# A timetable for the K stage, row tiles for half of Q, and the first denominators moved into gate/up

## The chip, the cores and the metric

The kernel runs on one core of a Trainium2 chip. The metric is the device time of one execution in microseconds; lower is better. A profile is one execution, of which the span (first to last instruction) is 1.7 to 1.8 us shorter than the device time. PE is TensorE, ACT is ScalarE, DVE is VectorE, POOL is GpSimd, SP is SyncE.

## The reference

```python
x  = A_x                                   # 1 x 2048 x 576, bf16
xn = layernorm(x)
# linear attention: 32 heads of 18
q, k, v = split_heads(xn @ wqkv)
phi = lambda t: where(t > 0, t + 1, exp(t)) + 1e-6
num = phi(q) @ (phi(k)^T v);  den = phi(q) . sum(phi(k)) + 1e-6
attention = (num / den) @ wo
# feed-forward with a gate
ffn = (gelu(x @ w_gate) * (x @ w_up)) @ w_down     # of xn
out = x + attention + ffn
```

## The kernel before

PE goes through these stages in order: K (layer norm, transposes, the K projection and G = xn^T phi(k), tile by tile), Q, then for each quarter of the rows gate/up and down. The first down stage begins with M, ten small matmuls that multiply the attention's kv by wo. PE writes into PSUM, which the kernel holds as one tile of 8 banks of 512 columns; a bank can be written again when ACT and DVE have read it. The change touches K, Q and the first gate/up stage.

In the K loop each tile n does the following; steps of tiles ahead are mixed in, and two tiles share one rstd from tile 7 on:

```python
for n in range(1, NS):
    if n > 1:
        k_half(n, 0); k_half(n, 1)               # PE: 10 matmuls of 288 columns
    if n + 1 < NS: tp_all(n + 1)                 # ACT: copy the transposes
    if n + 2 < NS and (n + 2 < PAIRED or n % 2 == 1):
        ln_rstd(n + 2, min(1 if n + 2 < PAIRED else 2, NS - n - 2))
    if n + 2 < NS: ln_norm(n + 2)                # DVE
    k_read(n, 0); k_read(n, 1)                   # ACT relu, DVE max, out of PSUM
    k_finish(n)                                  # ACT exp, POOL add -> pk
    ln_stats(...)                                # DVE
    if n >= GLAG: g_accumulate(n - GLAG, G_A)    # PE
    if n + 2 < NS: transposes(n + 2)             # PE
    if n in (NS - 2, NS - 1): q_unit(...)        # the first two units of Q
    # ... loads ...
```

phi is computed in two pieces that POOL adds. Both K and Q take the pieces from one small set of buffers, and Q has 20 units (4 row blocks x 5 groups of heads):

```python
def phi_tiles():
    e = awork.tile([P, D], F32, name="phi_e", tag="phi_e", bufs=3)
    a = awork.tile([P, D], F32, name="phi_a", tag="phi_a", bufs=2)
    return e, a

def q_unit(i):
    # ... 5 matmuls of 512 columns into one PSUM bank ...
    if i % 3 != 2:
        # ACT relu of the bank; DVE max of the bank into a; ACT exp; POOL add -> pqT
    else:
        # ACT exp of the bank; DVE max of the bank into a; DVE joins them -> pqT
```

The contraction is 576 rows, 4.5 times the array. Gate/up already uses row tiles so that the half block costs half a slot: two outputs are worked on at once, one in rows 0 to 63 of the array and one in 64 to 127, and they change places between `p1` and `p2`. A do-nothing instruction on another engine, the relay, passes on that the other row tile has written:

```python
def p1(self):
    for kt in (4, 0, 1, 2, 3):
        self.mm(0, LO, kt, kt == 4, False)
        last = self.mm(1, HI, kt, kt == 4, False)
    self.turn = self.relay.nop()      # waits for `last`
def p2(self):                         # first matmul waits for self.turn
    for kt in range(4): ...
```

The relay runs on GpSimd for all blocks of gate/up but the first two. That was so before the change already.

Of the kernel before, what the change touches and what calls it, by code (L numbers as in the profile page):

```python
# [40 lines left out]
PAIRED = 7  # L41
# [15 lines left out]
def kernel(  # L57
# [45 lines left out]

    def load_w(which):
        c = slice(which * D, (which + 1) * D)
        nc.sync.dma_start(wqkv_sb[:, 0:4, c], A_wqkv[0:512, c].rearrange("(kt p) c -> p kt c", p=P))
        nc.sync.dma_start(wqkv_sb[0:HP, 4, c], A_wqkv[512:576, c])

# [89 lines left out]
    ln_done = [0]  # L198

    def ln_stats(halves):  # L200

        while ln_done[0] < min(halves, 2 * NS):
            n, a_ = divmod(ln_done[0], 2)
            if a_ == 0:
                stats_t[n] = asmall.tile([P, 2, nc.vector.BN_STATS_DIM], F32, name="stats")
            nc.vector.bn_stats(out=stats_t[n][:, a_, :], in_=x_sb[:, n, a_ * HALF:(a_ + 1) * HALF])  # L206
            if a_ == 1:
                nc.vector.bn_aggr(out=mv[:, n, :], in_=stats_t.pop(n)[:])
            ln_done[0] += 1

    def ln_rstd(n, cnt=1):
        r = rstd[:, n:n + cnt]
        nc.scalar.activation(out=r, in_=mv[:, n:n + cnt, 1], func=ACT.Ln, bias=eps_ln[:], scale=1.0)  # L213
        nc.scalar.activation(out=r, in_=r, func=ACT.Exp, scale=-0.5)  # L214

    def ln_norm(n, dup=None):
        nc.vector.tensor_scalar(  # L217
            out=xn[:, n, 0:D], in0=x_sb[:, n, :], scalar1=mv[:, n, 0:1], scalar2=rstd[:, n:n + 1],
            op0=ALU.subtract, op1=ALU.mult,
        )  # L220
        (dup or nc.gpsimd).tensor_copy(out=xn[:, n, D:640], in_=xn[:, n, 512:D])
# [7 lines left out]
    def tp_copy(n, k0, k1, copy):  # L229
        copy(out=xnT[:, k0:k1, n * P:(n + 1) * P], in_=tp_bank[:, k0:k1, :])  # L230
# [20 lines left out]
    def k_read(n, hf):  # L251
        if hf == 0:
            k_ea[n] = phi_tiles()
        e, a = k_ea[n]
        hs = slice(hf * HALF, (hf + 1) * HALF)
        src = ps_all[:, k_bank(n, hf), :HALF]
        nc.scalar.activation(out=e[:, hs], in_=src, func=ACT.Relu, scale=-1.0)
        nc.vector.tensor_scalar(
            out=a[:, hs], in0=src, scalar1=0.0, scalar2=EPS_ATT, op0=ALU.max, op1=ALU.add,
        )  # L260

    def k_finish(n):
        e, a = k_ea.pop(n)
        nc.scalar.activation(out=e[:], in_=e[:], func=ACT.Exp, scale=-1.0)  # L264
        nc.gpsimd.tensor_tensor(out=pk[:, n, :], in0=e[:], in1=a[:], op=ALU.add)  # L265
# [10 lines left out]
    def g_accumulate(n, pieces):  # L276
# [7 lines left out]

    vcopy, acopy = nc.vector.tensor_copy, nc.scalar.copy

    G_COPIES = {
        3: [(0, G_A, 0, acopy), (0, G_A, 1, vcopy), (2, G_A, 0, acopy), (2, G_A, 1, vcopy)],
        5: [(1, G_A, 0, acopy), (2, G_A, 2, vcopy)],
        6: [(4, G_A, 2, acopy), (1, G_A, 1, vcopy)],  # L290
        7: [(4, G_A, 0, acopy), (4, G_A, 1, vcopy)],
        14: [(3, G_B, 0, acopy), (3, G_B, 1, vcopy)],
    }

    def tp_all(n):
        tp_copy(n, 0, KT, acopy)

    q_next = [0]
# [4 lines left out]
    def q_unit(i):  # L303
# [3 lines left out]
        cs = slice(sc * SC, (sc + 1) * SC)  # L307
        ps = ps_all[:rows, q_banks.next(), :]
        for kt in range(KT):
            nc.tensor.matmul(  # L310
                ps, lhsT=wqkv_sb[:, kt, q0:q0 + rows], rhs=xnT[:, kt, cs],
                start=(kt == 0), stop=(kt == KT - 1),
            )
        e, a = phi_tiles()
# [51 lines left out]

    def den_mm(sc, c, bank):
# [3 lines left out]
        d = dwork.tile([P, SC], F32, name="den_sb", tag="den_sb", bufs=5)  # L371
        if sc == 0:
            nc.scalar.activation(out=d[:rows, :], in_=ps, func=ACT.Identity, bias=eps_att[:rows, :], scale=1.0)
        else:
            nc.vector.tensor_scalar_add(out=d[:rows, :], in0=ps, scalar1=EPS_ATT)
        den_sb[c] = d

    def den_norm(sc, c, q, pieces):
        w = SC // pieces
        rows = DH * HCH[c]  # L380
        d = den_sb[c][:rows, q * w:(q + 1) * w]
# [8 lines left out]

    ln_stats(2)
    ln_rstd(0)
    ln_stats(3)
    ln_norm(0, nc.vector)
    transposes(0)
    ln_stats(4)
    tp_copy(0, 0, KT, vcopy)
    ln_rstd(1)
    k_half(0, 0)
    ln_norm(1)  # L400
    transposes(1)
    ln_stats(6)
    k_half(0, 1)
    k_read(0, 0)
    tp_all(1)
    ln_rstd(2)
    ln_stats(7)
    k_half(1, 0)
    ln_norm(2)
    k_read(0, 1)  # L410
    k_finish(0)
    transposes(2)
    k_half(1, 1)
    ln_stats(9)


    for n in range(1, NS):

        if n > 1:
            k_half(n, 0)  # L420
            k_half(n, 1)
        if n + 1 < NS:
            tp_all(n + 1)
        if n + 2 < NS and (n + 2 < PAIRED or n % 2 == 1):
            ln_rstd(n + 2, min(1 if n + 2 < PAIRED else 2, NS - n - 2))
        if n + 2 < NS:
            ln_norm(n + 2)
        k_read(n, 0)
        k_read(n, 1)
        k_finish(n)  # L430
        ln_stats(2 * (n + 4) + (1 if n < PAIRED - 4 else 2))
        if n >= GLAG:
            g_accumulate(n - GLAG, G_A)
        if n + 2 < NS:
            transposes(n + 2)
        if n in (NS - 2, NS - 1):
            q_unit(q_next[0])
            q_next[0] += 1
        if n == 2:
            load_x(8, 4)  # L440
        elif n == 3:
            load_x(12, 4)
        elif n == 5:
            load_w(0)
        elif n == 6:
            load_w(2)
        elif n == 7:
            load_wo()
        elif 8 <= n < 8 + NWBUF:
            load_gu(n - 8, 0)  # L450
            load_gu(n - 8, 1)
# [8 lines left out]
    for i in range(2, NSC * NCH):  # L460
        if i == 8:
            q_banks = _Ring([2, 3, 4, 5, 6, 7])
        q_unit(i)
        if i < 2 + GLAG:
            g_accumulate(NS - GLAG + i - 2, G_A)
        for kt, pieces, part, copy in G_COPIES.get(i, ()):
            g_copy(kt, pieces, part, copy)
        if i == 10:
            z_stage()
        if 5 <= i < 13:  # L470
            for n in (2 * (i - 5), 2 * (i - 5) + 1):
                g_accumulate(n, G_B)
        if 13 <= i < 13 + NCH:
            den_mm(0, i - 13, q_banks.next())
        if i == 17:
            kv_stage()
    scales = []
# [17 lines left out]



    LO, HI = slice(0, HP), slice(HP, P)
    SYNC = mybir.DependencyInfo(mybir.DependencyClass.Sync, mybir.DependencyReason.DATA)
    banks = _Ring(list(range(8)))  # L500

    class _Unit:


        def __init__(self, outs, lhs, rhs, relay=nc.gpsimd):
            self.outs, self.lhs, self.rhs, self.relay = outs, lhs, rhs, relay

        def mm(self, i, rows, kt, start, stop):
            return nc.tensor.matmul(  # L509
                self.outs[i], lhsT=self.lhs(i, rows, kt), rhs=self.rhs(i, rows, kt),  # L510
                start=start, stop=stop, skip_group_check=True,
            )

        def p1(self):
            for kt in (4, 0, 1, 2, 3):
                self.mm(0, LO, kt, kt == 4, False)
                last = self.mm(1, HI, kt, kt == 4, False)
            self.turn = self.relay.nop()
            tc.add_manual_dep(self.turn.ins, last.ins.name, SYNC, reason="the row tiles take turns on a bank")

        def p2(self):
            for kt in range(4):
                m = self.mm(1, LO, kt, False, kt == 3)
                if kt == 0:
                    tc.add_manual_dep(m.ins, self.turn.ins.name, SYNC, reason="the bank's other row tile has written")
                self.mm(0, HI, kt, False, kt == 3)

    def gu_pair(sc, k):
# [19 lines left out]
        if sc == 0 and k >= 1:  # L548
            load_wd_slice()
        for i, (b, u) in enumerate(units):  # L550
# [3 lines left out]
            nc.vector.tensor_tensor(out=hT[:, GUB * k + i, :], in0=ps_all[:, b[1], :], in1=gl[:], op=ALU.mult)  # L554

    m_banks = _Ring(list(range(2, 8)))

    def m_stage(chunks):
        for c in chunks:
            rows = DH * HCH[c]  # L560
            for hf in range(2):
                b = m_banks.next()
                hs = slice(hf * HALF, (hf + 1) * HALF)
                nc.tensor.matmul(  # L564
                    ps_all[:rows, b, :HALF], lhsT=kvT[:rows, c, :rows], rhs=wo2[:rows, c, hs], start=True, stop=True,
                )
                nc.scalar.copy(out=m_sb[:rows, c, hs], in_=ps_all[:rows, b, :HALF])

    def down_tile(sc, j, hooks):
# [4 lines left out]
        for hf in range(2):  # L574
            hs = slice(hf * HALF, (hf + 1) * HALF)
            todo = hooks.pop(0) if hooks else {}
            acc = ps_all[:, banks.next(), :HALF]
            for f in range(NF):
                if f in todo:
                    todo[f]()  # L580
# [14 lines left out]
    for sc in range(NSC):  # L595
        for k in range(NF // GUB):
# [3 lines left out]
            if den_jobs:  # L600
# [4 lines left out]
        hooks = [{6 * c_: (lambda c_=c_: m_stage((c_,))) for c_ in range(NCH)} if sc == 0 else {}]  # L605
        if sc + 1 < NSC:
            for c_ in range(NCH):
                def dn(c=c_, nsc=sc + 1):
                    den_mm(nsc, c, banks.next())
# [34 lines left out]
```

## Time and profile before

| | before |
|---|---|
| device time, median of the first 3 runs | 528.93 us (528.82 to 529.08) |
| PE busy | 520.7 us, 99% of the span |
| PE work after 12 us without a listed wait | all of it |
| Q unit 0 starts | 45.22 us |
| gate/up starts (first row-tiled matmul) | 77.75 us |
| first matmul of the M stage, at the start of down | 147.95 us |
| last matmul ends | 524.01 us |

The four times at the bottom are positions of PE in the trace. Here is the stretch at the end of K and the start of Q, from the chain in order of time of the kernel before (start, length, what):

```profile
45.38 1.09 PE ps_all L310 x5
46.47 1.23 PE ps_all L238 x10
47.70 0.98 PE ps_all L280 x10
48.68 2.17 PE ps_all L310 x10
50.86 0.99 PE ps_all L280 x10
51.84 1.09 PE ps_all L310 x5
52.94 0.99 PE ps_all L280 x10
```

Every piece starts where the one above ends, and each is a PE piece: Q unit 0 (L310), K of tile 15 (L238), G of tile 13, units 1 and 2, G of tile 14, unit 3, G of tile 15. No other engine holds PE up.

### The profile page before, as it was taken

To read this page: it belongs to the slowest core of one execution; us is meant where nothing else is said; L and a number is where in the kernel's file an instruction comes from. 1 tells how busy PE (TensorE), PEld (TensorE's weight loads), DVE (VectorE), ACT (ScalarE), POOL (GpSimd) and SP (SyncE) were. 2 spreads that over 40 slices of the span, in tenths; PEclk is the share of its full clock that TensorE was granted. 3 is DMA by queue.
4 is the path that set the end of the run, shared out by engine and by line. 5 is a ranking of instruction groups with operands and counts; after the bars stand their busy time and mean duration, and the time that the engine had idled before them with its cause. 6 is when DMAs were issued, how large, how long until landed. Compare 5 with 4: busy or idle time off the path is not lost.

```text
span 527.1 us, 10752 instructions
## 1 busy us (share of the span) xinstructions
PE 520.7 (99%) x4532; PEld 326.2 (62%) x4532; DVE 248.7 (47%) x408; ACT 152.8 (29%) x288; POOL 70.3 (13%) x83
## 2 busy tenths in 40 slices
PE   7999999999999999999999999999999999999997
PEld 5887666666677764444577744444777544445775
DVE  7885766774348613334368233433485233333101
ACT  5887783332330003233200023323000132322000
POOL 4666542210002100000011000000021000000000
PEclk9999999999999999999999999999999999999999
DMA  8900006999510025555400055455100345540000
GB/s 277 278 10 1 1 1 173 265 269 265 154 46 12 24 79 154 158 145 156 135 12 13 12 168 158 141 158 154 46 24 12 102 143 159 149 136 1 12 12 22
DMA packets 98810, 55.85 MB, mean 106 GB/s; under 512 B 5322, under 2 KB 98378, under 8 KB 98762
## 3 DMA queue, kind: packets, MB, share of 16 engines
q1 hardware_dynamic: 98762, 55.17, 36.2%
q8 instruction: 35, 0.57, 0.5%
q14 instruction: 13, 0.11, 0.1%
HBM read 52.79 MB, written 2.36 MB: 105 GB/s over the span
## 4 chain that ended last, share of the span: by engine, by line
PE 98%; DVE 1%; ACT 1%; DMA 0%; issue 0%
PE ps_all L509 53%; PE ps_all L581 27%; PE ps_all L310 4%; PE ps_all L586 4%; PE ps_all L280 4%; PE ps_all L238 3%; PE ps_all L227 1%; PE ps_all L370 1%; DMA x_sb<-in_A_x_dram 0%; ACT xnT L230 0%; PE ps_all L564 0%; PE ps_all L358 0%; DVE xn L217 0%; DVE stats L206 0%; ACT rstd L213 0%; ACT rstd L214 0%
## 5 line engine op out<-in xcount | busy, mean ns | idle before, releaser
L509 PE MATMUL ps_all<-xnT,wg 64*128 64x512 bf16 x1152 | 272.8, 376 | 0.0
L509 PE MATMUL ps_all<-xnT,wu 64*128 64x512 bf16 x1152 | 268.4, 376 | 0.0
L554 DVE TENSOR_TENSOR hT<-ps_all,gl 128x512 bf16<-128x512 f32 x144 | 99.5, 691 | 166.3 <-ACT gl L553 165.9
L553 ACT ACTIVATE gl<-ps_all 128x512 f32<-128x512 f32 x144 | 86.0, 597 | 313.5 <-PE ps_all L509 289.2
L581 PE MATMUL ps_all<-wd_sb,hT 128*128 128x288 bf16 x1152 | 147.0, 286 | 0.0
L509 PEld LDWEIGHTS <-wg 64*128 64x128 bf16 x1152 | 108.2, 94 | 62.6 <-issue 0.3
L509 PEld LDWEIGHTS <-wu 64*128 64x128 bf16 x1152 | 107.4, 94 | 61.8
L581 PEld LDWEIGHTS <-hT 128*128 128x128 bf16 x1152 | 112.3, 98 | 30.7 <-issue 1.3
L384 DVE RECIPROCAL den_sb<-den_sb 126x128 f32<-126x128 f32 (+1 forms) x80 | 68.3, 911 | 0.5
L387 POOL TENSOR_TENSOR pqT<-pqT,den_sb 126x512 bf16<-126x512 bf16 (+3 forms) x25 | 24.1, 964 | 298.5 <-DVE den_sb L384 295.2
L509 PE MATMUL ps_all<-xnT,wr 64*128 64x512 bf16 x288 | 60.6, 376 | 0.0
L589 DVE TENSOR_TENSOR res<-ps_all,x_sb 128x288 bf16<-128x288 f32 x32 | 14.6, 457 | 87.5 <-PE ps_all L586 87.5
L509 PEld LDWEIGHTS <-wr 64*128 64x128 bf16 x288 | 17.1, 94 | 16.3 <-issue 1.1
L586 PE MATMUL ps_all<-m_sb,pqT 126*128 126x288 bf16 (+1 forms) x160 | 24.9, 286 | 0.0
L310 PE MATMUL ps_all<-xnT,wqkv_sb 128*126 128x512 bf16 (+1 forms) x100 | 24.4, 380 | 0.0
L265 POOL TENSOR_TENSOR hT<-phi_e,phi_a 128x576 bf16<-128x576 f32 x16 | 22.4, 1402 | 8.9 <-ACT phi_e L264 4.9
L280 PE MATMUL ps_all<-hT,xn 128*128 128x288 bf16 (+3 forms) x192 | 23.6, 266 | 0.0
L238 PE MATMUL ps_all<-wqkv_sb,xnT 128*128 128x288 bf16 x160 | 22.5, 286 | 0.7 <-DVE xnT L230 0.6
L280 PEld LDWEIGHTS <-xn 128*128 128x128 bf16 (+1 forms) x192 | 18.2, 101 | 4.5
L320 POOL TENSOR_TENSOR pqT<-phi_e,phi_a 126x512 bf16<-126x512 f32 (+1 forms) x14 | 17.7, 1267 | 15.5 <-DVE phi_a L318 11.8
L586 PEld LDWEIGHTS <-pqT 126*128 126x128 bf16 (+1 forms) x160 | 15.5, 97 | 4.1
L238 PEld LDWEIGHTS <-xnT 128*128 128x128 bf16 x160 | 15.0, 98 | 4.6 <-DVE xnT L230 0.8
(58 smaller groups left out, 201.3 us busy)
## 6 DMA issues: line engine op xcount, KB each, us to landing
wg<-in_B_w_gate_dram SPq DMA_DIRECT2D x72, 256.0 KB, 2.9
wu<-in_B_w_up_dram SPq DMA_DIRECT2D x72, 256.0 KB, 3.4
wd_sb<-in_B_w_down_dram SPq DMA_DIRECT2D x12, 432.0 KB, 4.4
wr<-in_B_w_gate_dram SPq DMA_DIRECT2D x72, 32.0 KB, 2.7
wr<-in_B_w_up_dram SPq DMA_DIRECT2D x72, 32.0 KB, 3.0
out_dram<-res SPq DMA_DIRECT2D x15, 144.0 KB, 1.8
x_sb<-in_A_x_dram SPq DMA_DIRECT2D x3, 576.0 KB, 6.6
wqkv_sb<-in_A_wqkv_dram SPq DMA_DIRECT2D x2, 576.0 KB, 8.9
```

Of the source, the lines that this page charges most:

```text
L238: nc.tensor.matmul(ps_all[:, k_bank(n, hf), :HALF], lhsT=xnT[:, kt, n * P:(n + 1) * P], rhs=wqkv_sb[:, kt, D + hf * HALF:D + (hf + 1) * HALF],
L265: nc.gpsimd.tensor_tensor(out=pk[:, n, :], in0=e[:], in1=a[:], op=ALU.add)
L280: nc.tensor.matmul(ps_all[:m, b, col:col + w], lhsT=xn[:, n, j0:j0 + m], rhs=pk[:, n, d0:d0 + w], start=(n == 0 and col == 0), stop=(n == ...
L310: nc.tensor.matmul(ps, lhsT=wqkv_sb[:, kt, q0:q0 + rows], rhs=xnT[:, kt, cs], start=(kt == 0), stop=(kt == KT - 1),)
L320: nc.gpsimd.tensor_tensor(out=pqT[:rows, c, cs], in0=e, in1=a, op=ALU.add)
L384: nc.vector.reciprocal(out=d[:, h:h + P], in_=d[:, h:h + P])
L387: nc.gpsimd.tensor_tensor(out=pqT[:rows, c, cols], in0=pqT[:rows, c, cols], in1=d, op=ALU.mult)
L509: return nc.tensor.matmul(self.outs[i], lhsT=self.lhs(i, rows, kt), rhs=self.rhs(i, rows, kt), start=start, stop=stop, skip_group_check=True,)
L553: nc.scalar.activation(out=gl[:], in_=ps_all[:, b[0], :], func=ACT.Gelu_apprx_tanh)
L554: nc.vector.tensor_tensor(out=hT[:, GUB * k + i, :], in0=ps_all[:, b[1], :], in1=gl[:], op=ALU.mult)
L581: nc.tensor.matmul(acc, lhsT=hT[:, f, j * P:(j + 1) * P], rhs=wd_sb[:, f, hs], start=(f == 0), stop=False,)
L586: nc.tensor.matmul(acc, lhsT=pqT[:rows, c, ts_], rhs=m_sb[:rows, c, hs], start=False, stop=(c == NCH - 1),)
```

## The change

The intent is to make PE's work shorter in Q and its start denser:

- K gets a timetable. Each step has a time for each tile, and all steps are issued in the order of these times. rstd is no longer paired.
- The second half of Q is done in five pairs of units with the row tiles of gate/up, with relays on SP.
- The first six denominators leave Q (and one the first down stage) and are done in three row-tiled pairs inside gate/up.
- To make room, the second part of G and the z and kv stages (which make the denominators' and M's weights) move forward to units 5 to 8 of Q, and G of tiles 14 and 15 comes one unit later.
- The relays on GpSimd stay as they are.

The diff, cut to its core:

```diff
+    TILE = 2.5
+    STEPS = [
+        (lambda n: ln_half(n, 0), [3.02, 3.99, 6.44, 7.41, 9.44]),
+        ...
+        (lambda n: k_half(n, 0), [6.86, 8.09, 10.30, 13.01, 15.56]),
+        ...
+        (k_exp, [8.73, 11.12, 13.29, 15.61, 18.10]),
+        (k_add, [9.59, 11.73, 14.01, 16.29, 19.88]),
+    ]
+    todo = [(at(times, n), step, n) for n in range(NS) for step, times in STEPS]
+    todo += [(at(STEPS[7][1], NS - 1) - 0.01, q_unit, 0), (at(G_AT, NS - GLAG) - 0.01, q_unit, 1)]
+    todo += [(at(STEPS[-1][1], 4 + n) + 0.01, lambda n: nc.gpsimd.memset(pqT[HP:P, NCH - 1, ...], 0.0), n)
+             for n in range(2)]
+    ...
+    for _, step, n in sorted(todo, key=lambda x: x[0]):
+        step(n)
...
-    for i in range(2, NSC * NCH):
+    for i in range(2, 2 * NCH):
...
+    q_banks = _Ring(list(range(8)))
+    for k, items in enumerate([[(2, 0), (2, 1)], [(2, 2), (2, 3)], [(2, 4), (3, 4)], [(3, 0), (3, 1)], [(3, 2), (3, 3)], None]):
+        if items:
+            u = q_pair(items)
+            u.p1()
+        if prev:
+            prev[1].p2()
+            ...  # q_phi of the two units
...
+    DEN_FROM = 2
+    DEN_PAIRS = [[(0, 0), (0, 1)], [(0, 2), (0, 3)], [(0, 4), (1, 4)]]
...
-        if sc == 0:
-            nc.scalar.activation(out=d[:rows, :], in_=ps, func=ACT.Identity, bias=eps_att[:rows, :], scale=1.0)
-        else:
-            nc.vector.tensor_scalar_add(out=d[:rows, :], in0=ps, scalar1=EPS_ATT)
+        nc.vector.tensor_scalar_add(out=d[:rows, :], in0=ps, scalar1=EPS_ATT)
```

## The prediction

> **What bounds the kernel now.** I read the page's busy shares and chain first, then the waits of PE, the chain in order of time, and the timeline of three stretches. The first lines are the page's first part and the chain that ended last.
>
> ```profile
> PE 520.7 (99%) x4532; PEld 326.2 (62%) x4532; DVE 248.7 (47%) x408; ACT 152.8 (29%) x288; POOL 70.3 (13%) x83
> PE 98%; DVE 1%; ACT 1%; DMA 0%; issue 0%
> ```
>
> PE is busy 99% of the span, and the chain that sets the end runs on it for 98%. All the waits of PE that the trace lists come to 3.1 us:
>
> ```profile
> PE ps_all L132 <- POOL ident masks.py:199: 1.4, 1, 1.4
> PE ps_all L227 <- DVE xn L217: 1.1, 1, 1.1
> PE ps_all L238 <- DVE xnT L230: 0.6, 1, 0.6
> ```
>
> So almost nothing is to be had by removing listed waits. What can shorten the time is less PE work, or a denser start, where PE also has dead time that is put down to pipelining. The chain in order of time shows the K stage (columns: start, length, what):
>
> ```profile
> 12.19 1.23 PE ps_all L238 x10
> 13.42 0.98 PE ps_all L280 x10
> ...
> 21.91 0.52 PE ps_all L227 x5
> 22.43 1.25 PE ps_all L238 x10
> 23.68 0.98 PE ps_all L280 x10
> 24.66 0.33 PE ps_all L227 x5
> ```
>
> A tile of K is transposes (L227), ten K matmuls (L238) and ten accumulations of G (L280): at best 0.28 + 1.23 + 0.98 = 2.49 us. In every second tile the transposes take 0.52 instead of 0.28, because they wait for a norm that waits for the paired rstd. G of tile 0 starts at 13.4, of tile 12 at 44.4: 12 tiles in 31.0 us, 2.58 each, so 1.1 us above the best in steady state. Before 12 us PE is mostly idle: from its first transpose at 5.31 to 12.03 it does four groups of transposes and four K halves, 4 x 0.28 + 4 x 0.61 = 3.6 us of work in 6.7 us. So a perfect start could give some 3.1 us, a perfect steady state 1.1.
>
> **What the Trainium skill says.** (1) "TensorE: Matmul & The Clock Gate", Back-to-back issue gap: an isolated 512-column matmul takes about N / 2.4 + 2.5, some 216 ns, and a stream about 131. Here the starts of plain 512-column matmuls (L310) and those of pairs of row tiles (L509) stand 216 to 217 ns apart (648 matmuls of L509 in 70.2 us is 216.7 ns a pair). The trace agrees with the first figure, not with the second. (2) The same page, Weight-path perf modes: fast weight load needs 128 columns. The trace agrees: 98 ns for 128 columns (L581), 132 ns for 126 (L310). (3) "TensorEngine Tiling (Array Packing)", Gotcha 1: PSUM Pressure: row tiles may not use one PSUM bank at once and software must order them. That is what the relay between the two halves of a unit is for. (4) "PSUM — Partial Sum Buffer", PSUM bank collisions: no two engines may be in one bank (and quadrant) together. The trace agrees in effect: in Q, DVE's read of a bank starts only after ACT's (relu 46.57 to 47.17, maximum from 47.27), so a bank of Q comes free some 1.7 us after its last matmul was issued: 0.25 + 0.6 + 0.1 + 0.7.
>
> **The change part by part.**
>
> Row-tiled second half of Q. Now 10 units of 5 matmuls, 50 x 0.2165 = 10.8 us, the fifth of which uses half of the rows. Then 5 pairs of 9 slots (five in the first half, four in the second), 45 x 0.2165 = 9.7 us. Gain 1.1 us, if a slot keeps its length. The weight loads are 126 columns wide, 132 ns each. Two in one slot would be 264 ns if they excluded each other. In gate/up the two loads of a pair start in the same hundredth of a microsecond and still take 94 ns each, so I take it that they run side by side.
>
> ```profile
> 79.02 0.09 PEld L509 LDWEIGHTS <-wg 64*128 64x128 bf16 x1 [0.29 <-issue]
> 79.02 0.09 PEld L509 LDWEIGHTS <-wu 64*128 64x128 bf16 x1
> ```
>
> Denominators. Five matmuls of 0.22 leave Q (-1.1 us), three pairs of two slots enter gate/up (6 x 0.2165 = +1.3), and one later denominator of the down stage is done by then (-0.2). Sum 0. The five ACT copies of denominators (L373, 676 ns) leave ACT, and six DVE ones (L375, 680 ns) enter gate/up. In those blocks of 4.3 us DVE has two products (1.4), two copies (1.4) and from the second on two reciprocals (1.8), 4.6 us. It falls behind by at most 0.6 us for two blocks and catches up in the next, which has no copies (3.2 of 3.9 us). A bank is needed again about 2.2 us after its matmuls ended, and ACT and DVE need 1.3, so PE should not notice.
>
> K timetable. It puts both statistics of tile 1 before the norm of tile 0, and from then on has each step at the time at which its input should be there. I read the diff's own times as a claim. The first tile landed at 3.14 here and the statistics start at 3.02 in the timetable, so I add 0.14. Then G of tile 0 starts at 11.96 (before: about 13.2, by matmul starts) and of tile 4 at 22.30 (before 23.5): 1.2 us earlier, not 3.1, since the first three norms and transposes cannot come much sooner (the transposes of tile 3 at 11.67, before 11.66). From there 2.5 a tile against 2.58 gives 0.6 more up to tile 12. Is 2.5 possible? Effective spacings of ACT in a tile of before: Ln 0.33, Exp 0.11, two relus 0.73, exp 0.59, copy 0.57, sum 2.33, now with Ln and Exp in every tile, 93% of 2.5. DVE: statistics 0.98, norm 0.4, two maxima 0.75, sum 2.1. It fits, with 0.17 us of room on ACT. Gain 1.6 us, 1.8 by the timetable with something taken off for jitter.
>
> New waits at the end of K and in Q. Here the diff moves work in ways that a timetable of PE does not show. I followed the order of the engines with the durations above, from T, the start of Q unit 0.
> - Unit 0 now stands before the exponential of tile 14 on ACT and before that tile's addition on POOL. Its relu cannot start before T + 1.35, its maximum ends at T + 2.7, POOL's addition (1.27) at T + 4.1. Tile 15 needs its phi_a buffer, so its first maximum ends at T + 4.5, and unit 2, which needs that bank, would have started at T + 4.4. Wait 0.2 us, more if POOL starts late (in the trace of before this addition started 0.6 after its inputs).
> - POOL's addition of tile 15 ends around T + 9.0, G of tile 15 would start at T + 8.6 to 8.9: about 0.2. The copies of G, the last of them in units 6 and 7, free banks 2 and 3 about 0.1 late each for units 7 and 8: 0.2.
> - Unit 9 is in bank 2, and so is the second pair, 1.1 us later. Before unit 9's maximum DVE has unit 8's two operations and the two masks of z and kv. Counted from the end E of unit 8's matmuls: maximum E + 0.95, product E + 1.67, masks of z E + 2.4 to 3.15, of kv E + 3.15 to 3.9, unit 9's maximum until E + 4.6. PE gets to the second pair at E + 0.26 + 1.32 + 1.08 + 1.08 = E + 3.74. Wait 0.9 us. The lines of the masks and of a unit's maximum in before:
>
> ```profile
> 77.55 0.67 DVE L330 TENSOR_TENSOR kvT<-ps_all,bmask 126x504 bf16<-126x504 f32 x1
> 78.14 0.22 DVE L335 TENSOR_TENSOR kvT<-ps_all,bmask 72x72 bf16<-72x72 f32 x1
> 73.11 0.68 DVE L318 TENSOR_SCALAR phi_a<-ps_all 126x512 f32<-126x512 f32 x1
> ```
>
> Sum of new waits 1.5 us. Sum of all: -1.6 - 1.1 + 0 + 1.5 = -1.2, so 527.7. I shade it to 527.4, since the waits at T and at tile 15 partly cover each other: what delays PE there lets POOL catch up.
>
> **The rivals.** (a) The new waits do not come, or are hidden. Then -1.6 - 1.1 gives 526.2, with a full timetable gain of 2.3 even 525.5. For it: PE waits nowhere in Q before, with ACT 98% busy at 70 to 75 us. Against it: the bank of the second pair is a plain conflict, 1.1 us apart. (b) The pairs of Q bind on the weight loads: 45 slots of 264 instead of 216.5 ns, +2.1, 529.6. For it: 132 ns loads without fast loading. Against it: the loads that start together in gate/up. (c) ACT becomes the bound of K: with 2.33 busy of 2.5 and every relu timed to its bank, a tile of 2.6 eats the gain in steady state and half of the start's, 528.6. (d) The free phi_a buffer is taken the other way around, unit 2 waits for tile 15's addition, and DVE's copies of G come 1 us late: 528.6. (e) POOL or SP relays late inside gate/up, through DVE's backlog: a relay has about 0.9 us of room at the worst block, so at most a few tenths.
>
> **Range and chances.** The terms: K 0.6 to 2.4, Q 1.1 or -1.0, waits 0.3 to 3. Most of the mass lies between all waits hidden (525.3) and one rival of cost (529.3). 2% is 10.6 us. All of K, Q and the start that the change touches lasts 78 us, and none of it is near such a gain. A slowdown of that size would need a wait in each of the 72 blocks of gate/up, for which nothing speaks. So within 2% at 0.98, faster 0.01, slower 0.01.
>
> **What would show it.** In the profile after: 4578 matmuls (Q +40, denominators +6). The first G matmul near 12.0 us and that of tile 4 near 22.3. Every tile's transposes at 0.3 or so. Pairs of Q 217 ns apart in their slots; 264 shows (b). Among the waits of PE new ones for DVE's phi_a in Q, the longest about 0.9 us right after the first p1 of a pair; if none is listed there, (a) holds. Gate/up of the first 512 rows 70.2 + 1.3 us long; longer shows (e). The later three down and gate/up stages unchanged. The prediction is wrong if time is gained or lost after about 150 us.

## The result, and the profile after

| | before | after |
|---|---|---|
| device time, median of 6 runs | 528.83 us (528.76 to 529.08) | 528.67 us (528.52 to 529.64) |
| ratio | | 1.000 (0.9987 to 1.0012) |
| PE matmuls | 4532 | 4578 |

The ratio is the mean time of one kernel's runs over the mean of the other's in the same rounds, so it is not quite the ratio of the two medians. The time is the same. The scatter is not: before spans 0.3 us here, after 1.1. (Over all calls 43 of the 44 runs of before lie between 528.72 and 529.10; the other is the one of 530.44.)

The same views as before, of the profile after. First the busy shares and the chain that ended last:

```profile
PE 521.3 (99%) x4578; PEld 317.0 (60%) x4578; DVE 252.1 (48%) x414; ACT 150.7 (29%) x290; POOL 70.2 (13%) x85
PE 93%; ACT 2%; DVE 2%; POOL 2%; issue 1%; POOLq 0%; DVEq 0%; ACTq 0%
```

PE is still busy 99%, but it carries only 93% of the chain. Some 7% of the way to the end now leads through ACT, DVE and POOL. The waits of PE (in total, times, longest) say where:

```profile
PE ps_all L321 <- DVE phi_a L382: 0.7, 1, 0.7
PE ps_all L227 <- DVE xnT L231: 0.6, 1, 0.6
PE ps_all L321 <- DVE phi_a L376: 0.4, 1, 0.4
PE ps_all L239 <- DVE phi_a L260: 0.2, 1, 0.2
```

Two row-tiled matmuls (L321) wait for maxima of Q. The list leaves out short waits. For all of them I take the start of each matmul from the trace and subtract the usual spacing (216 ns for 512 columns); "gap" is that excess from here on. The gaps from 15 us on that before does not have, in the first profile after: 0.31 before Q unit 2, 0.16 before G of tile 15, 0.21 inside the next G accumulations, 0.51 at the second pair of Q, 0.86 in the second block of gate/up, and twice 0.13 within transposes at 23 and 26 us. They sum to 2.3 us.

The stretch of the first of them, in the chain in order of time of the profile after:

```profile
45.14 1.11 PE ps_all L349 x5
46.33 0.61 ACT phi_e L375
47.03 0.70 DVE phi_a L376
47.87 1.27 POOL pqT L378
49.13 1.38 POOL hT L271
50.53 0.70 DVE phi_a L376
```

After Q unit 0 (L349) the chain leaves PE: relu, maximum, POOL's addition of unit 0, POOL's addition of tile 14, the next maximum. In before the same stretch was all PE. The gap before unit 2 itself comes from the maxima of tile 15, of which the first frees the bank of unit 2. They need the buffer of unit 0, and DVE waits 1.45 us for POOL's addition of that unit:

```profile
49.17 0.82 DVE L260 TENSOR_SCALAR phi_a<-ps_all 128x288 f32<-128x288 f32 x2 [1.45 <-POOL pqT L378]
```

The largest gap is in gate/up. In the chain of before the first gate/up stage is one unbroken piece of PE, in that of after PE carries it only from the second block on:

```profile
77.82 70.20 PE ps_all L509 x648
```

```profile
82.67 66.44 PE ps_all L321 x612
```

The same gap, in the timeline (start, length, engine, what, idle time before it and what ended that):

```profile
80.62 2.50 POOL L378 TENSOR_TENSOR pqT<-phi_e,phi_a 126x512 bf16<-126x512 f32 x2 [1.29 <-ACT phi_e L377]
81.92 0.69 DVE L382 TENSOR_SCALAR phi_a<-ps_all 126x512 f32<-126x512 f32 x1 [0.85 <-POOL pqT L378]
82.67 0.37 PE L321 MATMUL ps_all<-xnT,wr 64*128 64x512 bf16 x1 [0.70 <-DVE phi_a L382]
```

The last unit of Q needs its maximum before its bank is free. The maximum needs one of the two phi_a buffers, and that is free only when POOL has added an earlier unit. DVE stands idle 0.85 us for it, and gate/up, already in its second block, waits for the bank.

There is a second effect. The first K matmuls of this profile, and the second to third five of before (its first five, from 6.61 us, have the same spacing):

```profile
7.20 3.74 PE L239 MATMUL ps_all<-wqkv_sb,xnT 128*128 128x288 bf16 x15
```

```profile
7.70 1.65 PE L238 MATMUL ps_all<-wqkv_sb,xnT 128*128 128x288 bf16 x10
```

Fifteen in 3.74 us against ten in 1.65. In the first, 288 columns are spaced 240 ns up to 10.8 us, in the second 122: PE runs at half rate for the first K tiles of this execution. The page's clock row shows full speed there, but it cannot tell: the trace's own record of the granted clock has its first entry at 10.75 us (in before at 6.39). This execution was also the slowest of the six (529.64).

### The profile page after: what moved, and what is told of

Same layout as the page of the kernel before. It is cut to its first block, busy times and chain, and to the rows that moved or that the text cites. A ratio compares the mean times of both kernels' runs of the same rounds, so it can differ in the third digit from the quotient of the medians. Undisturbed runs are those within 1.5% of the kernel's fastest.

```text
span 527.9 us, 10848 instructions
## 1 busy us (share of the span) xinstructions
PE 521.3 (99%) x4578; PEld 317.0 (60%) x4578; DVE 252.1 (48%) x414; ACT 150.7 (29%) x290; POOL 70.2 (13%) x85
## 4 chain that ended last, share of the span: by engine, by line
PE 93%; ACT 2%; DVE 2%; POOL 2%; issue 1%; POOLq 0%; DVEq 0%; ACTq 0%
PE ps_all L321 53%; PE ps_all L623 27%; PE ps_all L628 4%; PE ps_all L239 3%; PE ps_all L286 3%; POOL pqT L378 1%; PE ps_all L227 1%; PE ps_all L349 1%; PE ps_all L136 1%; DVE phi_a L376 1%; PE ps_all L434 1%; DVE phi_a L382 1%; ACT phi_e L375 0%; ACT phi_e L377 0%; ACT phi_e L256 0%
## 5 line engine op out<-in xcount | busy, mean ns | idle before, releaser
L321 PE MATMUL ps_all<-xnT,wg 64*128 64x512 bf16 x1152 | 272.6, 376 | 0.0
L321 PE MATMUL ps_all<-xnT,wu 64*128 64x512 bf16 x1152 | 268.5, 376 | 0.0
L321 PEld LDWEIGHTS <-wg 64*128 64x128 bf16 x1152 | 108.2, 94 | 68.9 <-issue 1.1
L321 PEld LDWEIGHTS <-wu 64*128 64x128 bf16 x1152 | 107.0, 94 | 67.1
L321 PE MATMUL ps_all<-xnT,wr 64*128 64x512 bf16 x288 | 61.9, 376 | 0.7 <-DVE phi_a L382 0.7
L321 PEld LDWEIGHTS <-wr 64*128 64x128 bf16 x288 | 17.1, 94 | 17.1 <-issue 0.7
L239 PE MATMUL ps_all<-wqkv_sb,xnT 128*128 128x288 bf16 x160 | 25.9, 301 | 0.3 <-DVE phi_a L260 0.2
L378 POOL TENSOR_TENSOR pqT<-phi_e,phi_a 126x512 bf16<-126x512 f32 (+1 forms) x13 | 16.3, 1266 | 19.3 <-DVE phi_a L376 16.7
L260 DVE TENSOR_SCALAR phi_a<-ps_all 128x288 f32<-128x288 f32 x32 | 14.3, 451 | 7.1 <-ACT phi_e L256 5.4
```

The costliest lines, as they stand in the source:

```text
L239: nc.tensor.matmul(ps_all[:, k_bank(n, hf), :HALF], lhsT=xnT[:, kt, n * P:(n + 1) * P], rhs=wqkv_sb[:, kt, D + hf * HALF:D + (hf + 1) * HALF],
L321: return nc.tensor.matmul(self.outs[i], lhsT=self.lhs(i, rows, kt), rhs=self.rhs(i, rows, kt), start=start, stop=stop, skip_group_check=True,)
L378: nc.gpsimd.tensor_tensor(out=pqT[:rows, c, cs], in0=e, in1=a, op=ALU.add)
```

## The experiments

Each has five rounds (experiment 2 has six times) with before run beside it on the same chip, on four chips. "Before" was 528.90 us in the first, 528.81 in the second and third and 528.86 in the last. The run of 530.44 fell in the first; without it the ratios of experiments 1 to 4 would be higher by some 0.0003 (an estimate from the means).

### 1. The changed kernel again

No edit.

> The changed kernel unchanged, for a second profile and more times. In the first profile its first 14 K matmuls are spaced 240 ns instead of 122, until 10.7 us; in the profile of before the same matmuls run at 122 from 6.7 us on. Theory A: when PE reaches its full rate varies from run to run, and that profiled run (529.64, the slowest of six) was an unlucky one. Then a second profile can show the step elsewhere, the times scatter by about 1 us again (528.5 to 529.6), and where the step comes early G of tile 4 starts near 22.9 instead of 23.9. Theory B: the change itself keeps PE at half rate until 10.7 us; then this profile shows the same step at 10.7 and every run pays for it.

Measured: 528.92 us (528.51 to 529.67), ratio 0.9999 (0.9988 to 1.0011). The same matmuls in the second profile:

```profile
7.18 2.11 PE L239 MATMUL ps_all<-wqkv_sb,xnT 128*128 128x288 bf16 x15
```

The step to full rate now comes at 7.2 us, not 10.8: the clock record starts at 7.17, and the first K matmuls are spaced 122 (one spacing of 230 ns at 7.9 is a single wait, before the second half of tile 0). G of tile 4 starts at 22.96 (before 23.52, first profile after 23.91). All gaps from 15 us on are the same within 0.02 us, and the last matmul ends at 523.93 against 524.87. So theory A holds: the half rate at the start changes from run to run, and the 0.94 us that it cost in the first profile stay to the end. In the clock records of all 14 profiles the full rate begins between 4.17 and 7.17 us, but for the first profile after, at 10.75, so that one is the exception. That the scatter of all the times comes from it is not shown. From here on I use this second profile as the profile after.

Where the gain went, from these two traces:

| position of PE | before | after (2nd profile) | gained since start | by this stage |
|---|---|---|---|---|
| Q unit 0 | 45.22 | 44.02 | 1.20 | +1.20 |
| gate/up | 77.75 | 75.68 | 2.07 | +0.87 |
| M stage | 147.95 | 148.09 | -0.14 | -2.21 |
| end | 524.01 | 523.93 | 0.08 | +0.22 |

In Q the work falls by 1.1 (row tiles) and 1.1 (denominators), and 1.3 of that is lost in gaps. In gate/up the denominators come back (+1.3), and the 0.87 gap is added. In down one denominator is saved.

### 2. More dummy matmuls at the start

```diff
-NWARM = 36
+NWARM = 38
+    def warm(n):            # between the transposes of tiles 0 and 1
+        if n == 0:
+            for _ in range(6):
+                nc.tensor.matmul(ps_all[:, 4, 0:P], lhsT=ident[:], rhs=ident[:], start=True, stop=True)
```

> The changed kernel with 8 more dummy matmuls in the idle gaps of the start: 2 more of the warm-up, and 6 between the transposes of tiles 0 and 1, where PE waits 0.6 us for a copy. Theory A (half rate until PE was busy without a break for long enough, so the gaps of the start decide): no 240 ns spacing after about 8.3 us in the profile, a time 0.3 to 1.0 us under the changed kernel's mean and less scatter. Rival: the dummies only add work in a gap: the same times within 0.3 us, and the step can come as late as 10.7 us again.

Measured: 528.71 us (528.11 to 529.34), ratio 0.9995 (0.9983 to 1.0007). This profile has no K matmul at 240 ns, as expected of theory A, but the profile of experiment 1 had none either, and the step comes at 7.16 us here and 7.17 there. Neither the mean nor the scatter changed beyond doubt. The dummies did not help; what sets the moment of the step stays open.

### 3. The timetable alone

The kernel before, with the changed kernel's K stage and nothing else.

> The kernel before with the timetable of K alone; Q and the denominators as before. Theory (the new waits at the end of K eat part of a small gain): Q unit 0 starts 0.3 to 1.3 us sooner than in before (45.2), according to PE's rate at the start, and PE then waits about 0.3 us before Q unit 2 on DVE's phi_a; time 0.0 to 0.9 us under before, 528.3 in the middle. Rival (the prediction's timetable gain is real and Q lost it): 1.6 us under before, 527.2.

Measured: 528.86 us (528.76 to 529.15), ratio 0.9998 (0.9986 to 1.0009). Q unit 0 starts at 43.66, 1.56 us sooner than in before. So the timetable does gain. But all of it is lost within 10 us; the timeline, with the addition of tile 15 and G of tile 15:

```profile
50.05 1.26 POOL L318 TENSOR_TENSOR pqT<-phi_e,phi_a 126x512 bf16<-126x512 f32 x1 [0.87 <-DVE phi_a L316]
51.27 1.41 POOL L267 TENSOR_TENSOR hT<-phi_e,phi_a 128x576 bf16<-128x576 f32 x1
52.73 1.15 PE L282 MATMUL ps_all<-hT,xn 128*128 128x288 bf16 x10 [1.05 <-POOL hT L267]
```

POOL does Q unit 1 before tile 15, and PE waits (gap 1.21 us) for tile 15. With the 0.31 before unit 2 that is 1.52, the gain to within 0.05. Gate/up starts at 77.70, in before at 77.75. The expectation was right on the time and the first wait, and missed the second, larger one. In the changed kernel G of tile 15 stands one Q unit later, behind unit 4; its wait there is only 0.15.

### 4. The row tiles and denominators alone

The changed kernel with the K loop of before; the three memsets on POOL stay within the K loop.

> The changed kernel with the K stage of before; only the row-tiled Q and the denominators in gate/up. Theory (Q's gain of 1.1 us is given back by two waits, 0.5 us at the second pair and 0.9 us in the second block of gate/up, and the denominators cost 0.0): within 0.5 us of before, 528.8 to 529.3, with both waits in the profile. Rival (the waits come from the timetable's timing and Q alone is a gain): 1.1 us under before, 527.7, and neither wait.

Measured: 529.46 us (529.41 to 529.77), ratio 1.0010 (0.9998 to 1.0022). Both waits are there, 0.52 at the second pair and 0.88 in gate/up, so they do not come from the timetable. It is somewhat slower than expected, since the K loop has gaps of 0.43 and 0.33 us at 22.4 and 25.6, at POOL's two memsets (0.52 and 0.57 us). Beside the first memset DVE's norm takes 0.72 us, against 0.43 for the same norm in experiment 11, which has no memset there; the transposes wait for it. The second memset pushes POOL's copy of columns that a transpose needs:

```profile
21.63 0.72 DVE L222 TENSOR_SCALAR xn<-x_sb,mv,rstd 128x576 bf16<-128x576 bf16 x1 [0.60 <-ACT rstd L219]
24.68 0.57 POOL L512 MEMSET pqT<- 64x512 bf16 x1
25.32 0.24 POOL L226 COPY xn<-xn 128x64 bf16<-128x64 bf16 x1
```

### 5. Three phi_a buffers

```diff
-        a = awork.tile([P, D], F32, name="phi_a", tag="phi_a", bufs=2)
+        a = awork.tile([P, D], F32, name="phi_a", tag="phi_a", bufs=3)
```

> The changed kernel with three phi_a buffers in place of two. Theory (Q's maxima wait for POOL's additions only because they share two buffers): the 0.86 us wait in the second block of gate/up, the 0.31 before Q unit 2 and the 0.15 before G of tile 15 go, the 0.51 at the second pair stays; time 1.0 to 1.4 us under the changed kernel, 527.5. Rival (POOL's additions, 1.27 us each, are the bound of that stretch themselves): the wait in gate/up moves by less than 0.2 us, and the time is within 0.4 us of the changed kernel's.

Measured: 528.52 us (527.63 to 528.66), ratio 0.999 (0.9978 to 1.0003). The gap in gate/up falls from 0.87 to 0.08 and the one before unit 2 goes, so the buffers were the cause of both. But the gain was 0.3 to 0.4, which isn't clear of noise, and not 1.0 to 1.4: with the first wait gone PE comes to G of tile 15 sooner and waits longer there (0.64 in place of 0.15), and a denominator pair in gate/up gets a gap of 0.47. The waits of PE name the two:

```profile
PE ps_all L286 <- POOL hT L271: 0.5, 1, 0.5
PE ps_all L321 <- SPq L330: 0.3, 1, 0.3
```

The second is the relay on SP. The pair's relay stood in the queue behind the issues of two loads, the first of which held SP for 2.03 us:

```profile
85.62 2.03 SPq L173 DMA_DIRECT2D wr<-in_B_w_up_dram  x1
87.69 0.59 SPq L556 DMA_DIRECT2D wd_sb<-in_B_w_down_dram  x1
```

### 6. Other banks for the pairs

```diff
-    q_banks = _Ring(list(range(8)))
+    q_banks = _Ring([0, 1, 4, 5, 6, 7, 2, 3])
-    banks = _Ring([2, 3, 4, 5, 6, 7, 0, 1])
+    banks = _Ring([4, 5, 6, 7, 2, 3, 0, 1])
```

> The changed kernel with the pairs of Q in banks 0,1 4,5 6,7 2,3 0,1, so that the second pair no longer takes the bank of Q unit 9; the ring of gate/up turned along with it. Theory (that wait is a bank conflict): the 0.51 us wait at the second pair goes. What becomes of it: if POOL's chain of additions sets the later wait in gate/up, that chain starts when the first pair ends, which is 0.5 sooner, so the time falls by 0.3 to 0.5, to 528.3. Rival (the later wait is fixed by something that began before the pairs): the wait in gate/up grows from 0.86 to 1.3 and the time stays.

Measured: 529.43 us (529.18 to 530.4), ratio 1.0014 (1.0002 to 1.0027). The gap at the second pair is gone, the one in gate/up is 0.82, as the theory has it, and gate/up starts 0.53 us sooner than in experiment 1. But the time grew, through a fault of my edit: the M stage counts its banks from the accumulator's by adding 2 and more, and along the turned ring these fall on banks that the last gate/up block has just filled. Two gaps of 0.84 and 0.60 stand there at 148.3 and 149.0 us. The run shows that the bank was the cause of the wait; what it is worth it doesn't show (experiment 12 does).

### 7. The memsets at POOL's idle start

```diff
+    for n in range(2):      # right after the other constants
+        nc.gpsimd.memset(pqT[HP:P, NCH - 1, n * SC:(n + 1) * SC], 0.0)
+    nc.gpsimd.memset(zrep[HP:P, NCH - 1, :], 0.0)
```

and the same three taken out of the timetable.

> The changed kernel with its three POOL memsets (zero rows for the half-row tiles) moved from inside the K stage to POOL's idle start. Theory (each of the two larger ones, 0.52 us, delays a copy of POOL that a transpose waits for): the 0.135 us gaps in the transposes at 22.3 and 24.9 go, Q unit 0 starts 0.27 us sooner; time 0.0 to 0.3 under the changed kernel, less if the later waits take it back. Rival: the gaps have another cause and stay.

Measured: 528.41 us (528.24 to 528.82), ratio 0.9993 (0.998 to 1.0006). The gaps in the transposes are gone, Q unit 0 starts at 43.66 (44.02 in experiment 1), and the last matmul ends 0.38 us sooner. The time agrees with that but is not clear of noise. The theory had the right culprit and the wrong path. The POOL queue of experiment 1:

```profile
21.17 0.52 POOL L495 MEMSET pqT<- 64x512 bf16 x1
21.98 0.24 POOL L221 COPY xn<-xn 128x64 bf16<-128x64 bf16 x1 [0.30 <-DVE xn L215]
```

The memset was over 0.30 us before the copy began: the copy waited for DVE's norm of the same tile. Beside the two memsets that norm took 0.67 and 0.81 us; here, with POOL idle at that time, it takes 0.38 both times. (In before it takes 0.83 to 0.86 us where POOL's addition runs beside it for most of the time, and 0.43 where POOL is idle.) The two gaps make 0.27 of the 0.36 us at Q unit 0.

### 8. All four together

Experiments 2, 5, 6 and 7 in one kernel.

> The changed kernel with all four: three phi_a buffers, the other banks for the pairs, the memsets at the start, the dummy matmuls in the start's gaps. Theory (the change's gain is real and was eaten by these waits): the gaps of PE after 12 us that before does not have fall from 2.5 us to under 0.7, and the time is 2.0 us under before, 526.9, an interval clear of it. Rival (each wait removed gives way to the next): within 0.7 us of before.

Measured: 528.59 us (528.26 to 528.65), ratio 0.9993 (0.998 to 1.0007). Not what was expected. Gate/up starts at 75.07, 2.7 us sooner than in before, with no gap in its first blocks. Then the M stage loses 1.45 us by the fault of experiment 6; its first two matmuls in the timeline:

```profile
147.40 0.28 PE L612 MATMUL ps_all<-wo,kvT 126*126 126x288 bf16 x1 [0.69 <-ACT gl L600]
148.13 0.28 PE L612 MATMUL ps_all<-wo,kvT 126*126 126x288 bf16 x1 [0.44 <-DVE hT L601]
```

They wait for the gelu (`gl`) and the product (`hT`) of the last gate/up block. G of tile 15 has its 0.64 gap.

### 9. All waits mended

Experiments 5, 6 and 7, without the dummies, and

```diff
+    def past(bank, n):
+        return RING[(RING.index(bank) + n) % 8]
-            b = (acc_bank + 2 + (2 * c + hf) % 6) % 8
+            b = past(acc_bank, 2 + (2 * c + hf) % 6)
-                        den_mm(nsc, c, (b + 2) % 8)
+                        den_mm(nsc, c, past(b, 2))
+    AHEAD = {(k_exp, NS - 2): 43.03, (k_add, NS - 2): 43.04}    # before Q unit 0
+    todo = [(AHEAD.get((step, n), t), step, n) for t, step, n in todo]
-    ... (at(G_AT, NS - GLAG) - 0.01, q_unit, 1)
+    ... (at(STEPS[-1][1], NS - 1) + 0.01, q_unit, 1)            # after POOL's addition of tile 15
```

> The changed kernel with the waits taken away and the previous run's own fault mended: three phi_a buffers, memsets at the start, the pairs of Q in other banks, the M stage's banks counted along the turned ring (with the turned ring alone they fell on banks of the last gate/up block and cost 1.45 us), and on ACT and POOL the last steps of K tiles 14 and 15 ahead of Q units 0 and 1. No dummy matmuls. Theory (the gain is there: 1.5 us from K, 1.1 from Q, and what eats it is these waits): between 12 and 150 us PE has no gap over 0.3 us but the one at the first K matmuls; down starts near 146.1, and the time is 526.4, 2.4 us under before. Rival (a new wait takes the place of each one removed): 528 or more.

Measured: 526.52 us (526.32 to 526.84), ratio 0.9957 (0.9944 to 0.9969). This is faster than before, beyond noise (by 0.4%), all five times are below every time of either kernel, and it is as expected. The chain of its Q and its gate/up is on PE again:

```profile
62.53 1.34 PE ps_all L424 x25
63.87 1.08 PE ps_all L357 x5
64.95 25.22 PE ps_all L329 x230
```

From the last single unit of Q (L357) on, 25 us of row tiles, pairs of Q and gate/up alike (both L329), pass without a break. Gate/up starts at 74.65 (3.10 sooner than in before), the M stage at 146.23 (1.72), the last matmul ends at 522.06 (1.95).

### 10. The timetable alone, with the order at its end mended

Experiment 3 with the three `AHEAD` and `q_unit` lines of experiment 9.

> The kernel before with the timetable of K, and on ACT and POOL the last steps of tiles 14 and 15 ahead of Q units 0 and 1. Theory (the timetable alone gained 1.56 us up to Q unit 0 and lost 1.5 in two waits for POOL: 0.31 before unit 2 and 1.21 before G of tile 15): the second goes, the first goes or stays under 0.2, gate/up starts near 76.3, time 527.4. Rival (POOL's additions catch up with PE elsewhere in Q): gate/up starts after 77.3 and the time is 528.4 or more.

Measured: 527.83 us (527.28 to 528.18), ratio 0.998 (0.9966 to 0.9994). Both gaps are gone, gate/up starts at 76.29 and the last matmul ends 1.47 us sooner than in before. So the order on POOL and ACT at the end of K was what ate the timetable's gain. The median gained 1.0, less than the trace does.

### 11. The row tiles alone, mended

Experiment 4 with the edits of 5, 6 and 7 and the `past` lines of 9.

> The K stage of before, row-tiled Q and denominators, with three phi_a buffers, the memsets at the start, and the other banks with the M stage's banks counted along. Theory (without its waits the row-tiled Q gains its 1.1 us, the denominators nothing): gate/up starts 2.0 to 2.2 us sooner than in before (77.75), 1.1 of it the denominators' that come back later, and the time is 527.8. Rival (row-tiled Q cannot gain since ACT and POOL set Q's length, and PE waits for them at its end): 528.6 or more with a wait in the first blocks of gate/up.

Measured: 528.17 us (527.81 to 528.83), ratio 0.9987 (0.9975 to 1.0). Gate/up starts at 75.73, 2.02 sooner than in before, without a wait, and the last matmul ends 0.87 sooner. The row-tiled Q gains its 1.1 us on the trace, less small losses; the interval of the times just reaches 1.

### 12. The mended kernel with the old banks

The two bank rings of experiment 9 set back to those of the change.

> The mended kernel (526.52 in the last call) with the banks of the changed kernel again: the second pair of Q takes the bank of unit 9. It isolates the bank conflict, whose run of its own was spoilt by the M stage's banks. Theory (a conflict of one bank, worth what PE waits there): one gap of 0.4 to 0.5 us before the second pair is back, and the time is 0.3 to 0.5 over the mended kernel, 526.9. Rival (what PE loses there it gets back at the next wait): 526.5, as mended.

Measured: 527.39 us (526.87 to 528.36), ratio 0.9975 (0.9961 to 0.9989). The gap is back; the maximum of unit 9 and the matmul that waits for it:

```profile
65.54 0.68 DVE L384 TENSOR_SCALAR phi_a<-ps_all 72x512 f32<-72x512 f32 x1
66.27 0.37 PE L329 MATMUL ps_all<-xnT,wqkv_sb 64*126 64x512 bf16 x1 [0.28 <-DVE phi_a L384]
```

The gap is 0.45 us, and the last matmul ends 0.31 later than in experiment 9. But Q unit 0 starts 0.19 sooner here; counted from there to the end the loss is 0.50. So, as the theory has it, what PE waits there is not won back. The median is 0.9 us higher, more than the trace accounts for; the two runs were on two chips and their intervals overlap, so for the size I go by the trace.

## Why the prediction was right or wrong

528.67 lies inside 525.3 to 529.3, and "within 2%" came true, which says little, since 2% is 10.6 us. The middle value was 1.3 us too low: the gain of 1.5 us that it forecast did not come (the ratio's interval, 0.9987 to 1.0012, is -0.7 to +0.6 us). The bound was right, and the terms of the sum were of different quality.

- **PE as the bound, nothing outside the first 150 us.** Right. Down and the later gate/up stages differ from before by the one denominator only.
- **The pairs of Q.** Right. A slot of a pair takes 216 ns with 126 columns too, so the weight loads, still 132 ns each, lie beside each other. Rival (b) is out. In experiment 9 the whole pair stage lasts from 64.88 to 74.65, 9.77 us; 45 slots of 0.2165 are 9.74.
- **The denominators.** Right: 1.1 us out of Q, 1.3 into gate/up, 0.2 out of down. The first gate/up stage grew by 2.2 us and not 1.3, which by the prediction's own signs would be rival (e), a late relay; it was the wait for phi_a. A late relay came only in experiment 5 (0.47).
- **The timetable's gain of 1.6.** Right by experiment 3, 1.56 at Q unit 0, though split another way. G of tile 4 starts at 22.76 there, not 22.30, so the start gives 0.76 and not 1.2; from there a tile takes 2.49 us and not 2.5, and the steady state gives 0.8 and not 0.6. One reason for the late start is in the trace after: at 8.05 us DVE's statistics of tile 3 have waited 0.43 us for its load, and the norm of tile 2 stands behind them. A tile of 2.49 also rules out rival (c). The full change kept only 1.20 of the 1.56. I had read the memsets in the diff and charged them to nothing; DVE's norm beside them took 0.67 and 0.81 us and not 0.38, and POOL's copy and the transposes came later. By experiment 7 moving them is worth 0.36.
- **The new waits, predicted as 1.5 us.** Right in kind, and for K and Q a little large in sum (1.2 measured). Before unit 2: 0.2 predicted, 0.31 measured, by the path predicted (the maximum of tile 15), so rivals (a) and (d) are out. G of tile 15: 0.2 and 0.15. Copies of G: 0.2 for units 7 and 8, and instead 0.21 at the first accumulation after tile 15. The second pair: 0.9 and 0.51, since PE got there 0.2 us later than worked out and the maximum ended 0.2 sooner.
- **The term that failed** is the sentence that in gate/up "PE should not notice". I had followed the banks of gate/up among themselves and DVE's load of denominators, and both were fine. I had not followed the last units of Q into it. Their maxima wait for a phi_a buffer from POOL, and so the bank of the last unit comes free only in the second block of gate/up. That is 0.86 us, shown by experiment 5, which takes it away with a third buffer. With it the waits come to 2.1 us, not 1.5.
- **The shading to 527.4,** because waits cover each other, went the wrong way. Experiment 5 shows what covering does: take one wait away and the next grows. That is a reason to expect little from mending one wait, and not a reason to expect a smaller sum.

So with a term for the wait in gate/up (0.86) and one for the memsets (0.36), and the waits in Q as measured (1.27 in sum with a small one of 0.08), the terms are -1.56 + 0.36 - 1.1 + 0 + 1.27 + 0.86 = -0.2 us. The last matmul of the second profile ends 0.08 sooner than in before, and the medians differ by -0.16; with a scatter of 1.1 us, that the medians fit so closely is luck. The intended gain was there and was given back: experiment 9 takes the waits away and gets 2.3 us of it by the medians, 1.95 by the traces.

## What to carry to other kernels

Here one engine was at 99%, and a reordering that made its own sequence denser was paid for on the others. In such a case write down the order on POOL, ACT and DVE at each seam between stages, and count the buffers and banks that cross it, since a timetable for the busy engine alone doesn't show them. Where a gain is missing, compare the positions of the bound engine at the stage borders of both traces; that told in one table which stage won and which lost. And mend all the waits of a seam together before judging: in experiment 5 most of what was removed went to other waits, though experiments 6 and 7 kept theirs on the trace (0.53 us up to gate/up, 0.38 to the end). Last, an operation put into idle time of one engine can lengthen its neighbour's: the norm on DVE took up to twice as long beside a memset on POOL.

## What the Trainium skill lacked or had wrong

- "TensorE: Matmul & The Clock Gate", Part 1: The HAM clock gate, says that what is issued in the first 3.4 us or so runs at half rate and everything after at the full one. Here, with 36 dummy matmuls from 1.4 to 5.1 us and then gaps of up to 0.9 us, the full rate began at 10.75 us in one execution, 9.3 us after the first matmul, and between 4.17 and 7.17 us in the other 13, 2.7 to 5.7 after it. The same section says that the moment varies from run to run, which agrees, but by 500 ns either way, and here two executions of one kernel lie 3.6 us apart. What puts it off in one run and not in another of the same kernel is not shown by any run, and experiment 2 did not settle it.
- The same page, Back-to-back issue gap: the stream figure of 131 ns for 512 columns is not reached in any stage; 216 to 217 ns, plain or in row-tiled pairs. That is the figure which the section gives for an isolated matmul.
- The same page, Part 3: Packing small matmuls, does not give the spacing of row-tiled pairs whose weights are too narrow for fast loading. With 126 columns and loads of 132 ns, a pair of 512 columns takes the same 216 ns as with 128 columns.
- "TensorEngine Tiling (Array Packing)", Key Properties, says that a change of tiling mode drains the engine, without a figure. Here the spacing at each change between whole and row-tiled matmuls grows by 0.09 to 0.10 us, eight times in the kernel.
- No page that I found warns that a do-nothing relay on SP stands in line behind the issue of loads: one issue held SP for 2.03 us and the next for 0.59, and a pair of matmuls had a gap of 0.47 us for it (experiment 5).
